# Strassen's seven products in the second feed-forward product of the last two token groups

## The chip, the cores and the metric

One core of one Trainium2 chip. The metric is the device time of one execution in microseconds (us), lower is better. In what follows PE is TensorE (its matmuls; PEld its weight loads), DVE is VectorE, ACT ScalarE, POOL GpSimd and SP SyncE, whose queue issues all the DMA transfers here. PSUM is the memory that matmuls write, eight banks of 512 float32 columns; SBUF is the working memory.

## The reference

Two branches on the same normalised input are added to the input: a spectral filter and a two-stage mixer.

```python
def _A_ref(x, w_r, w_i):                      # spectral filter
    X = rfft2(x)
    return irfft2(X * (w_r + 1j * w_i), (S, D))

def _B_ref(x, w1, w2, w3, w4):                # mixer
    h = gelu(layernorm(x) @ w1)               # then four channel quarters shifted by +1, -1, +2, -2 tokens
    x1 = x + concat(g0, g1, g2, g3) @ w2
    h2 = gelu(layernorm(x1) @ w3) @ w4        # the feed-forward part
    return x1 + h2

xn = layernorm(A_x)
out = A_x + _A_ref(xn, A_w_r, A_w_i) + _B_ref(xn, B_w1, B_w2, B_w3, B_w4)
```

There are S = 2048 tokens of D = 448 channels; w3 is 448 x 1792 (F = 1792), w4 is 1792 x 448. All is float32.

## The kernel before

**Precision.** Each float32 operand of a product is split into a high and a low half in float16 (a ScalarE copy gives the high half, a subtraction the low one), and a product is made of three passes: high by high, high by low, low by high (`PASS`). Powers of two from `powers` keep the halves in range.

**Tiles and groups.** The tokens are 16 tiles of 128 (b = 0 to 15, interleaved: token a * 16 + b). The feed-forward part works on groups G = 0 to 7 of two tiles each, 256 tokens.

**A unit.** For a group, the 1792 inner channels are taken in seven units fp = 0 to 6 of two blocks of 128 (f = 2 fp and 2 fp + 1). A unit has two halves.
- `front(G, fp)`: the product with w3 into one PSUM bank, [inner channel, token], by `mlp_in` (L381: 22 matmuls of 256 columns). Then Gelu in place in PSUM (L694, ScalarE), the high half (L696, ScalarE), the low half (L697, VectorE), into the tile `hf`.
- `back(G, fp)`: the product with w4, [token, output channel]; for each of the two token tiles and each of the two blocks three passes, added into the accumulators of the group, one bank for each tile (L716: 12 matmuls of 448 columns). In group 7 the second tile's accumulator is two halves of 224 columns in two banks, so its back is 6 matmuls of 448 and 12 of 224. At the group's last unit VectorE adds the accumulators to the residual (L728); for groups 6 and 7 (L723) it adds them to a row that already holds the rest of the output (`unscaled`, L493: a row of x loaded by SP, times and plus), and SP sends the result out (L725).

`mlp` runs the units of the groups that it is given, the front of a unit `ahead` units before its back (one for groups 3 to 7, two for 0 to 2).

**What else runs in the last 130 us.** The inverse transform, tile by tile: `gather_u` copies the transform's array `Y` of pool `pa2` for eight tiles into `U` (L651, VectorE, twice); `inv_a` has matmuls into a bank of tag `tr` (L659), a ScalarE copy (L663), two GpSimd sums (L666, L667), four VectorE sums (L668 to L671) and the split (L673, L674); `inv_b` is the second product (L681) and its addition to the tile (L682); `finish` loads a row of x, adds (L493) and sends the row out (L497).

**PSUM.** Four tags of two banks each: `mm` (fronts), `acc` (accumulators), `tr` (transposes, `inv_a`), `sp` (`inv_b` and group 7's third accumulator).

**SBUF.** `x2mem` holds the transposed input of all fronts (groups 0 and 1 in its first quarter, 2 and 3 in the second, 4 and 5, 6 and 7) and a strip behind them. `w4p` has the halves of w4. The four rows of groups 6 and 7 that hold the rest of the output lie in the first quarter.

**What sets the order.** The kernel text gives every engine's instructions with priorities: evictions first (`prio(EVAC)`), then the normal text in its order, feed-forward products last (`prio(FILL)`). A planner goes through them on a timeline of its own, takes on each engine the ready instruction of best priority, and so writes one fixed order for each engine, with all waits. On the chip, each engine goes through its order and waits where it must; nothing is reordered there.

## Time and profile before

| | us |
|---|---|
| time, median of 3 runs (lowest to highest) | 418.66 (418.37 to 418.75) |
| profiled execution: span from first to last instruction | 417.1 |
| median less span | 1.56 |
| PE busy | 408.7 (98%) |
| VectorE busy | 292.4 (70%) |
| ScalarE busy | 248.3 (60%) |
| GpSimd busy | 119.5 (29%) |
| L381, products with w3, 1232 matmuls | 152.2 |
| L716, products with w4, 714 matmuls | 140.0 |
| granted TensorE clock, mean | 0.999 |

For the profiled execution the page gives the span alone, so its own time is taken as the span and the 1.56 us around it. Matmuls are pipelined, so the busy times and mean durations of PE overlap each other; its pace is read from the starts of successive groups of matmuls. Times in a row of a timeline are the start and the length of a run of like instructions, in us from the start of the span; in brackets stands idle time of that engine ahead of the row and what ended it. In rows of groups, the two figures behind the first bar are the busy time in all (us) and the mean of one instruction (ns), behind the second bar the idle time ahead of them.

### The profile page before, as it was taken

Reading aid. Unit: us, or ns where it says so; the run is one execution under the profiler, and the core shown is the slowest. Engines: PE = TensorE matmul, PEld = TensorE weight load, DVE = VectorE, ACT = ScalarE, POOL = GpSimd, SP = SyncE. Lnnn points to the kernel's source line nnn. Section 1 sums busy time; section 2 is a strip of 40 time slices with the busy share of each in tenths; the row PEclk is TensorE's granted clock in tenths of the full one; section 3 lists DMA queues with packets and bytes.
Section 4 is the critical chain, followed back from the end, with each engine's and each line's share of the span. In section 5 each row is a group of like instructions: output and inputs, shape, how many; then the busy total and the mean of one; then the engine's idle time right before and its main releaser. Section 6 shows DMA issues by size and latency. Waiting matters only on the chain.

```text
span 417.1 us, 8522 instructions
## 1 busy us (share of the span) xinstructions
PE 408.7 (98%) x3313; PEld 290.1 (70%) x3313; DVE 292.4 (70%) x619; ACT 248.3 (60%) x428; POOL 119.5 (29%) x204
## 2 busy tenths in 40 slices
PE   8999999999999999999999999999999999999996
PEld 3655555765667777776887887777776767577885
DVE  4888899798774757643689889865999429942122
ACT  4698879963758866632678888864534415422321
POOL 3876810101246746300031221211354203200000
PEclk9999999999999999999999999999999999999999
DMA  8959879814961374305056565710002003331001
GB/s 269 344 196 176 159 152 328 158 45 96 214 135 45 90 259 142 110 24 140 13 154 168 144 150 139 181 33 2 2 2 75 14 2 133 134 132 46 2 0 46
DMA packets 55544, 48.53 MB, mean 116 GB/s; under 512 B 37648, under 2 KB 50768, under 8 KB 55504
## 3 DMA queue, kind: packets, MB, share of 16 engines
q1 hardware_dynamic: 55504, 47.99, 43.4%
q8 instruction: 26, 0.43, 0.4%
q14 instruction: 14, 0.11, 0.1%
HBM read 35.52 MB, written 3.67 MB: 94 GB/s over the span
## 4 chain that ended last, share of the span: by engine, by line
PE 63%; DVE 18%; DMA 6%; issue 6%; ACT 3%; POOL 2%; SPq 1%; DVEq 0%; POOLq 0%; ACTq 0%
PE pw L381 23%; PE acc L716 22%; PE pw L410 4%; PE ps L536 3%; PE pu L638 2%; PE pp L593 2%; PE px L610 2%; PE wps L752 2%; DVE xt L452 2%; DMA x2mem<-y 1%; DMA x2mem<-w 1%; DVE hf L697 1%; DMA xr<-x 1%; DVE y L484 1%; DMA out<-xr 1%
## 5 line engine op out<-in xcount | busy, mean ns | idle before, releaser
L381 PE MATMUL pw<-x2mem,w3p 128*128 128x256 f16 x1232 | 152.2, 272 | 0.0
L716 PE MATMUL acc<-w4p,hf 128*128 128x448 f16 (+1 forms) x714 | 140.0, 341 | 1.1 <-DVE hf L697 1.1
L381 PEld LDWEIGHTS <-w3p 128*128 128x128 f16 x1232 | 118.9, 98 | 23.5 <-issue 0.9
L716 PEld LDWEIGHTS <-hf 128*128 128x128 f16 x714 | 69.2, 98 | 49.4 <-DVE hf L697 1.9
L697 DVE SCALAR_TENSOR_TENSOR hf<-pw,h,hf 128x512 f16<-128x512 f32 x56 | 41.8, 747 | 56.4 <-ACT hf L696 56.1
L694 ACT ACTIVATE pw<-pw,pe 128x512 f32<-128x512 f32 x56 | 36.7, 655 | 69.9 <-PE pw L381 68.8
L450 PE MATMUL pw<-w2p,h 112*128 112x448 f16 x192 | 39.9, 352 | 0.9 <-DMA h<-hs 0.8
L696 ACT ACTIVATE hf<-pw,h 128x512 f16<-128x512 f32 x56 | 38.3, 686 | 1.4
L619 POOL TENSOR_TENSOR z<-te 128x450 f32<-128x450 f32 x16 | 16.3, 1016 | 74.0 <-DVE te L617 74.0
L410 PE MATMUL pw<-w1p,xT 128*128 128x448 f16 x176 | 35.4, 352 | 0.0
L450 PEld LDWEIGHTS <-h 112*128 112x128 f16 x192 | 18.6, 98 | 17.4 <-DMA h<-hs 1.1
L666 POOL TENSOR_TENSOR e<-e 128x226 f32<-128x226 f32 x16 | 13.8, 866 | 56.2 <-ACT e L663 45.0
L410 PEld LDWEIGHTS <-xT 128*128 128x128 f16 x176 | 17.0, 98 | 16.4 <-DVE xT L375 0.8
L600 ACT ACTIVATE pf<-pp 64x450 f16<-64x450 f32 x32 | 17.3, 541 | 16.6 <-DVE pf L601 8.1
L601 DVE TENSOR_TENSOR pf<-pp,pf 64x450 f16<-64x450 f32 x32 | 19.9, 621 | 5.3 <-ACT pf L600 5.0
L663 ACT ACTIVATE e<-pe 128x452 f32<-128x452 f32 x16 | 8.7, 548 | 15.9 <-DVE vh L674 11.9
L516 POOL TENSOR_TENSOR xr<-xf 128x452 f32<-128x452 f32 x8 | 9.5, 1194 | 28.5 <-issue 23.0
L615 ACT ACTIVATE te<-px 64x450 f32<-64x450 f32 x32 | 17.2, 539 | 0.5
L673 ACT ACTIVATE vh<-e 128x448 f16<-128x448 f32 x16 | 9.2, 574 | 13.3 <-DVE e L671 11.3
L519 POOL TENSOR_TENSOR f<-xr 128x452 f32<-128x452 f32 x16 | 16.1, 1029 | 0.6
L527 DVE TENSOR_TENSOR xh<-f,xh 128x452 f16<-128x452 f32 x16 | 11.8, 781 | 5.9 <-ACT xh L526 5.9
L681 PE MATMUL py<-vh,csm 128*128 128x448 f16 x48 | 13.5, 352 | 1.5 <-DVE vh L674 0.7
(166 smaller groups left out, 600.9 us busy)
## 6 DMA issues: line engine op xcount, KB each, us to landing
wc<-wf SPq DMA_DIRECT2D x32, 225.0 KB, 3.7
wl<-wf SPq DMA_DIRECT2D x8, 450.0 KB, 3.7
xt<-x SPq DMA_DIRECT2D x8, 448.0 KB, 8.5
xf<-x SPq DMA_DIRECT2D x8, 448.0 KB, 3.7
w3raw<-w SPq DMA_DIRECT2D x3, 896.0 KB, 12.9
xr<-x SPq DMA_DIRECT2D x12, 224.0 KB, 2.6
out<-xr SPq DMA_DIRECT2D x12, 224.0 KB, 2.0
gn<-c_g SPq DMA_DIRECT2D x16, 128.0 KB, 3.3
```

The lines of the kernel that those rows point to most:

```text
L381: T.matmul(ps_out, wp[:, wi + t, cols], xT[:, xi + t, tok], start=t == 0 and wi + xi == 0, stop=t == 3 and wi == 4)
L410: T.matmul(pm[:, :D], xTs[g][:, xi + t, 128 * i:128 * i + 128], w1p[:, wi + t], start=t == 0 and p == 0, stop=t == 3 and p == 2)
L450: T.matmul(pm[:, :D], hT[g][:112, 4 * hi + k, o:o + 128], w2p[:, wi, k], start=n == 0, stop=n == 11)
L519: P.tensor_tensor(out=f[:, :, k:k + 2].rearrange("p b s d -> p s b d"), in0=u[:, :, 0], in1=u[:, :, 1], op=op)
L600: A.activation(out=hi, in_=src, func=AF.Copy)
L601: V.tensor_tensor(out=lo, in0=src, in1=hi, op=ALU.subtract)
L615: A.activation(out=e[64 * h:64 * h + 64], in_=px_[64 - 64 * h:128 - 64 * h, :2 * DF], func=AF.Copy)
L619: P.tensor_tensor(out=z, in0=t[:, 0], in1=t[:, 1], op=ALU.add)
L694: A.activation(out=pm, in_=pm, func=AF.Gelu_apprx_tanh, scale=r3)
L696: i = A.activation(out=h[:, 0], in_=pm, func=AF.Copy, scale=h3)
L697: j = V.scalar_tensor_tensor(out=h[:, 1], in0=pm, scalar=h3, in1=h[:, 0], op0=ALU.mult, op1=ALU.subtract)
L716: m = T.matmul(to, h[:, hi, o:o + 128], w4p[0][:, wi, f, r], start=f == 0 and n == 0, stop=f == 13 and n == 2)
```

## The change

For eleven units (group 6: units 0 to 5; group 7: units 0 to 4) the back is a product of two by two blocks: two token tiles by two blocks of inner channels, times two blocks of inner channels by two halves of the output channels (`DH` = 224). It is done with seven products in place of eight, each in three passes: 21 matmuls of 224 columns.

- **Sums of activations** (`sums`): Gelu writes to SBUF in place of PSUM, GpSimd makes the sums (two instructions, 256 and 384 columns), and the split goes over seven blocks, 896 columns, in place of four.
- **Sums of weights** (`w4_sums`): for six units the two blocks of w4 are loaded from memory once more, GpSimd makes the four sums (three instructions), and they are split. The results go to parts of `x2mem` that groups 0 to 3 used, and to a strip behind `w4p`. Their working buffers are in a new pool `pz`, in the place of `pa2`, which is closed after the inverse transform's text.
- **Products** (`seven`): three of the seven go into the group's accumulators, four into two side banks of tag `tr`. After the group's last such unit VectorE adds the side banks, blocks repeated by a broadcast, to the rows of the output in five instructions; then the accumulators are evicted as before.
- **Order**: group 6 begins with its plain unit 6; group 7 ends with its plain units 5 and 6. `mlp` for groups 6 and 7 runs two fronts ahead in place of one. The rows that hold the rest of the output move to the input of groups 4 and 5, the third quarter of `x2mem`. `powers` leaves one bit more room for w4.

```diff
+DH = D // 2
+STR = {6: [6, 0, 1, 2, 3, 4, 5]}
+ORD = {G: STR.get(G, list(range(7))) for G in range(8)}
+SEVEN = {6: range(0, 6), 7: range(0, 5)}
...
@@ front
         with prio(EVAC):
+            if fp in SEVEN.get(G, ()):
+                hs[G, fp] = sums(G, fp, pm)
+                return
             A.activation(out=pm, in_=pm, func=AF.Gelu_apprx_tanh, scale=r3)
...
+    def sums(G, fp, pm):
+        g = pz.tile([128, 12, 128], F32, tag="g", bufs=2, name=f"g{G}{fp}")
+        q = g.rearrange("p (a r) n -> p a r n", r=3)
+        A.activation(out=q[:, 0:2, 0:3:2].rearrange("p t f n -> p f t n"),
+                     in_=pm.rearrange("p (f t n) -> p f t n", f=2, t=2), func=AF.Gelu_apprx_tanh, scale=r3)
+        P.tensor_tensor(out=q[:, 2:4, 0], in0=q[:, 0:2, 0], in1=q[:, 0:2, 2], op=ALU.add)
+        P.tensor_tensor(out=q[:, 0:3, 1], in0=q[:, 1:4, 0], in1=q[:, 0:3, 0], op=ALU.subtract)
+        h = pz.tile([128, 2, 7 * 128], F16, tag="hz", bufs=3, name=f"hz{G}{fp}")
+        src = g[:, 1:8].rearrange("p a n -> p (a n)")
+        A.activation(out=h[:, 0], in_=src, func=AF.Copy, scale=h3)
+        V.scalar_tensor_tensor(out=h[:, 1], in0=src, scalar=h3, in1=h[:, 0], op0=ALU.mult, op1=ALU.subtract)
+        return h
+
+    def w4_sums(j):
+        raw = pz.tile([128, 4, DH], F32, tag="wr", bufs=2, name=f"wr{j}")
+        SY.dma_start(raw.rearrange("p (f k) n -> p f (k n)", f=2), w4v[:, 2 * j:2 * j + 2])
+        t = pz.tile([128, 4, DH], F32, tag="wt", bufs=1, name=f"wt{j}")
+        P.tensor_tensor(out=t[:, 0:2], in0=raw[:, 1:4:2], in1=raw[:, 0:2], op=ALU.subtract)
+        P.tensor_tensor(out=t[:, 2], in0=t[:, 1], in1=raw[:, 0], op=ALU.add)
+        P.tensor_tensor(out=t[:, 3], in0=raw[:, 2], in1=t[:, 2], op=ALU.subtract)
+        split_w(w4t[j][:, 0], w4t[j][:, 1], t, s4)
+
+    def seven(G, fp):
+        h = hs.pop((G, fp))
+        f0, f1 = 2 * fp, 2 * fp + 1
+        if fp == SEVEN[G][0]:
+            side[G] = [bank("tr", f"side{G}{i}") for i in range(2)]
+        at1 = [acc[G][1][:, 0:DH], acc[G][2][:, 0:DH] if G == 7 else acc[G][1][:, DH:D]]
+        w = lambda f, k: [w4p[0][:, i, f, DH * k:DH * k + DH] for i in range(2)]
+        t = lambda k: [w4t[fp][:, i, k] for i in range(2)]
+        end = fp == SEVEN[G][-1]
+        for blk, to, b, first in ((2, side[G][0][:, 0:DH], w(f0, 0), True), (4, at1[0], w(f1, 0), None),
+                                  (1, acc[G][0][:, 0:DH], t(3), None), (6, at1[1], w(f1, 1), None),
+                                  (5, side[G][1][:, 0:DH], t(0), True), (3, side[G][0][:, DH:D], t(2), False),
+                                  (0, side[G][1][:, DH:D], t(1), False)):
+            for n, (hi, wi) in enumerate(PASS):
+                o = 128 * blk
+                m = T.matmul(to, h[:, hi, o:o + 128], b[wi], start=n == 0 and (first and fp == SEVEN[G][0] if first is not None
...
+        if end:
+            x = rest[2 * G][0].rearrange("p b (k n) -> p b k n", k=2)
+            m16, m57 = (t.rearrange("p (k n) -> p k n", n=DH) for t in (s[:, 0:D] for s in side[G]))
+            with prio(EVAC):
+                def add(to, m):
+                    V.scalar_tensor_tensor(out=to, in0=m, scalar=p34[:, 1:2], in1=to, op0=ALU.mult, op1=ALU.add)
+                flat4 = x.rearrange("p b k n -> p (b k) n")
+                wide = lambda m, n: m.unsqueeze(1).to_broadcast([128, n, DH])
+                add(flat4, wide(m16[:, 0], 4))
+                add(flat4[:, 0:2], wide(m16[:, 1], 2))
+                add(flat4[:, 3], m16[:, 1])
+                add(flat4[:, 1:4:2], wide(m57[:, 0], 2))
+                add(flat4[:, 0:2], wide(m57[:, 1], 2))
...
@@ mlp
-            todo = [(G, fp) for G in Gs for fp in range(7)]
+            todo = [(G, fp) for G in Gs for fp in ORD[G]]
...
-                if fp == 3 and last:
-                    for b in (2 * G, 2 * G + 1):
-                        rest[b] = unscaled(b, x2mem.bitcast(F32)[:, D * (b - 12):D * (b - 11)])
+                if fp == ORD[G][3] and last:
+                    both = x2mem.bitcast(F32)[:, D * (2 * G - 4):D * (2 * G - 2)].rearrange("p (b n) -> p b n", b=2)
+                    for i in range(2):
+                        rest[2 * G + i] = both, unscaled(2 * G + i, both[:, i])
...
-    w4p[0] = pa.tile([128, 2, 14, D], F16, tag="R", bufs=1, name="w4p")
+    w4mem = pa.tile([128, 8 * F], F16, tag="R", bufs=1, name="w4p")
+    w4p[0] = w4mem[:, 0:28 * D].rearrange("p (i f n) -> p i f n", i=2, f=14)
+    homes = [x2mem[:, F * k:F * k + F] for k in (0, 1, 2, 3, 8)] + [w4mem[:, 28 * D:28 * D + F]]
+    w4t.update({j: m.rearrange("p (i k n) -> p i k n", i=2, k=4) for j, m in enumerate(homes)})
...
-    mlp(range(6, 8), last=True)
+    close("pa2")
+    pz = pool("pz")
+    for j in range(6):
+        w4_sums(j)
+    mlp(range(6, 8), last=True, ahead=2)
```

37 lines of the change are left out of this document (23 added, 14 removed).

## Prediction

> **What bounds the kernel now.** The page was read first: its busy times, then the chain that ended last. After that came the table of busy times by stretch, the chain in order of time, and each engine's timeline around the last two token groups.
>
> ```profile
> span 417.1 us, 8522 instructions
> PE 408.7 (98%) x3313; PEld 290.1 (70%) x3313; DVE 292.4 (70%) x619; ACT 248.3 (60%) x428; POOL 119.5 (29%) x204
> 330.00:340.00 10.00, 10.00 (x76) 7.24 (x75) 1.56 (x3) 2.70 (x4) 0.00 (x0) 1.00 0.00 0
> 340.00:350.00 10.00, 10.00 (x72) 6.82 (x70) 7.16 (x12) 4.09 (x7) 0.33 (x1) 1.00 0.23 72
> 350.00:360.00 10.00, 10.00 (x89) 7.31 (x87) 9.17 (x20) 3.84 (x7) 6.00 (x8) 1.00 0.39 139
> 360.00:370.00 10.00, 9.58 (x65) 5.95 (x64) 7.84 (x19) 3.74 (x6) 0.00 (x0) 1.00 0.49 161
> 380.00:390.00 10.00, 10.00 (x83) 7.80 (x81) 2.69 (x4) 2.70 (x4) 0.00 (x0) 1.00 0.12 46
> ```
>
> The last five rows are ten-microsecond stretches: PE, PE loads, VectorE, ScalarE and GpSimd busy, granted clock, DMA. PE is full through nearly all of the last 75 us. VectorE's load is quite uneven: idle at 330 to 340, three quarters to nine tenths busy while the inverse transform's last tiles run (340 to 370), idle again behind that. So work taken off PE here shortens the kernel unless something new makes PE wait, and the stretch to fear is 340 to 370.
>
> The chain in order of time (start, length, what) gives PE's pace without the pipeline's overlap:
>
> ```profile
> 381.11 2.27 PE acc L716 x12
> 383.38 2.40 PE pw L381 x22
> 385.79 2.29 PE acc L716 x18
> 409.22 4.58 PE acc L716 x36
> ```
>
> A front (L381) is 22 products in 2.40 us. A back of group 6 is 12 products of 448 columns in 2.27 us, 189.2 ns each. In group 7 it is 6 of 448 and 12 of 224 in 2.29 us, so a product of 224 columns takes (2.29 - 6 x 0.1892) / 12 = 0.0962 us; the last 36, of which 12 are wide, give the same.
>
> The page's span is 417.1 us, the median of the runs 418.66: 1.56 us lie outside the span, and I carry them unchanged. From no change this measurement can tell about 0.2%, 0.84 us.
>
> **The products.** Eleven units (six of group 6, five of group 7) get seven products of blocks in three passes: 21 products of 224 columns, 21 x 0.0962 = 2.02 us. Group 6 gains 0.25 us in each, group 7 gains 0.27: 6 x 0.25 + 5 x 0.27 = 2.85 us, all of it on PE and on the path. The front is untouched. That is all that the change can win; everything else in it is cost.
>
> One thing could take this from the products: each brings a weight load of its own (98 ns in the groups' rows), now behind only 224 columns.
>
> ```profile
> L716 PEld LDWEIGHTS <-hf 128*128 128x128 f16 x714 | 69.2, 98 | 49.4 <-DVE hf L697 1.9
> 352.55 1.18 PE L659 MATMUL pe<-csm,U 113*128 113x113 f16 x20
> 353.57 1.15 PE L381 MATMUL pw<-x2mem,w3p 128*128 128x256 f16 x9
> ```
>
> The inverse transform's products take a load each too, and 20 of them start within 353.57 - 352.55 = 1.02 us, 51 ns apart. So loads overlap one another, and at 96 ns they do not set the pace. The Trainium skill, "TensorE: Matmul & The Clock Gate", section "LDWEIGHTS (loading the stationary operand)", puts a load at its columns over 1.2 per ns, an estimate of 106.7 ns for 128. If loads of that length were the pace, a unit would take 2.24 us and the gain would shrink to 6 x 0.03 + 5 x 0.05 = 0.43 us. The 51 ns speak against that.
>
> **The sums of activations.** A unit's eviction was Gelu, Copy and a subtraction of 512 columns. It becomes Gelu, two sums on GpSimd (256 and 384 columns), Copy and subtraction of 896 columns.
>
> ```profile
> L697 DVE SCALAR_TENSOR_TENSOR hf<-pw,h,hf 128x512 f16<-128x512 f32 x56 | 41.8, 747 | 56.4 <-ACT hf L696 56.1
> L694 ACT ACTIVATE pw<-pw,pe 128x512 f32<-128x512 f32 x56 | 36.7, 655 | 69.9 <-PE pw L381 68.8
> L696 ACT ACTIVATE hf<-pw,h 128x512 f16<-128x512 f32 x56 | 38.3, 686 | 1.4
> L666 POOL TENSOR_TENSOR e<-e 128x226 f32<-128x226 f32 x16 | 13.8, 866 | 56.2 <-ACT e L663 45.0
> L519 POOL TENSOR_TENSOR f<-xr 128x452 f32<-128x452 f32 x16 | 16.1, 1029 | 0.6
> L264 ACT ACTIVATE w4p<-x2mem,pe 128x896 f16<-128x896 f32 x7 | 6.8, 1030 | 2.7 <-DVE pe L251 2.7
> L265 DVE SCALAR_TENSOR_TENSOR w4p<-x2mem,pe,w4p 128x896 f16<-128x896 f32 x7 | 7.9, 1137 | 0.0
> ```
>
> Before: 0.66 + 0.69 + 0.75 = 2.1 us from front to back. After: Gelu 0.66, the sums 0.9 and 0.98 (between the rows of 226 and 452 columns), Copy 1.03, subtraction 1.14: 4.7 us. With two fronts ahead, two fronts and two backs lie between (2 x (2.40 + 2.02) = 8.8 us), so it is hidden; with one ahead, 4.4 us would not have hidden it, and every unit would have lost 0.3 us. Each unit adds 1.9 us to GpSimd, 0.34 to ScalarE, 0.39 to VectorE.
>
> **The sums of weights.** Six times: load 448 KB, three GpSimd sums (448, 224, 224 columns: 1.03 + 2 x 0.87 = 2.8 us), ScalarE 1.03, VectorE 1.14. The buffer between them is single, so they run one after the other, 5.0 us each, 30 us in all. They start when the pool they live in is free, that is when the second gather has read the transform's array.
>
> ```profile
> 308.65 2.77 DVE L651 COPY U<-y 113x1024 f16<-113x1024 f16 x8
> xf<-x SPq DMA_DIRECT2D x8, 448.0 KB, 3.7
> L493 DVE SCALAR_TENSOR_TENSOR x2mem<-xt,s,x2mem 128x448 f32<-128x448 f32 x4 | 3.2, 790 | 0.0
> 339.31 1.80 PE L381 MATMUL pw<-x2mem,w3p 128*128 128x256 f16 x15
> 355.12 2.24 PE L716 MATMUL acc<-w4p,hf 128*128 128x448 f16 x11
> ```
>
> From 311.4 + 3.7 = 315 us they need until 345 if nothing delays them, across VectorE's empty stretch at 330; their loads sit in SP's queue ahead of the row loads of the output, 3.7 us for each, where the DMA engines are mostly idle. The first is wanted near 355, where the second back of group 6 runs now (355.12), the others 4.4 us apart. So they cost nothing on PE while that stretch stays empty; at worst the last two slide behind 345. The four residual rows of groups 6 and 7 (L493 on x2mem, 4 x 0.79 = 3.2 us of VectorE) do move into the crowded stretch: their new place is the input of groups 4 and 5, which fronts read until shortly before 339.31, where the first front of group 6 stands.
>
> **VectorE and GpSimd meet.** On VectorE's and GpSimd's timelines:
>
> ```profile
> 311.82 0.96 POOL L667 TENSOR_TENSOR e<-e 128x226 f32<-128x226 f32 x1
> 312.27 1.00 DVE L674 TENSOR_TENSOR vh<-e,vh 128x448 f16<-128x448 f32 x1
> 313.93 0.74 DVE L697 SCALAR_TENSOR_TENSOR hf<-pw,h,hf 128x512 f16<-128x512 f32 x1
> 313.99 0.58 POOL L666 TENSOR_TENSOR e<-e 128x226 f32<-128x226 f32 x1 [1.20 <-ACT e L663]
> 315.37 0.61 DVE L674 TENSOR_TENSOR vh<-e,vh 128x448 f16<-128x448 f32 x1
> ```
>
> An L674 beside a GpSimd sum takes 1.00 us, alone 0.61: 0.39 us for each meeting. L697, which reads PSUM, takes 0.74 beside one too. The change moves that subtraction's input from PSUM to SBUF, so it becomes of the first kind. The Trainium skill, "SBUF — State Buffer", section "Who interferes with whom", says that a VectorE instruction with two SBUF inputs and a reading GpSimd instruction shut each other out for a whole instruction; the rows agree as to which instructions are hit, and by that rule a meeting could cost the whole 0.96 us of L667 in place of 0.39, and the 16 meetings below 15.4 us.
>
> For 340 to 370 VectorE has 7.16 + 9.17 + 7.84 = 24.2 us of work. To it come 3.2 (residual rows), five units x 0.39 = 2.0, and two late sums of weights, 2.3: 31.7 us in 30. With all 16 new GpSimd instructions there (five units of two, two of three) meeting one each, 6.2 more: 37.9. So the surplus is 1.7 to 7.9 us. The inverse tail, whose last output leaves at about 371, may end near 379, far ahead of the end; it is on the path only where PE waits in its written order, or where group 6's side sums wait for the two banks of the last inverse tile. To go on with, PE has the back of unit 6 and the fronts of units 2 and 3, about 7 us. PE waited 0.42 us in this stretch (10.00 - 9.58). On the gain side, taking the residual rows away from 298 to 313 could give back PE's waits there, seen in its timeline as 0.34 and 0.75 us (the third row is the inverse tail's last output):
>
> ```profile
> 298.60 0.54 PE L681 MATMUL py<-vh,csm 128*128 128x448 f16 x2 [0.34 <-ACT vh L673]
> 313.32 0.35 PE L681 MATMUL py<-vh,csm 128*128 128x448 f16 x1 [0.75 <-DVE vh L674]
> 369.52 1.51 SPq L497 DMA_DIRECT2D out<-xr  x2
> ```
>
> The price of this part lies between -1.1 and +4.8 us (the middle of the surplus, unhidden). I take +0.6, near the 0.42 that PE waits today, since fronts can fill in.
>
> **From group 6 to group 7.** Behind group 6's last product VectorE has five additions, then the two evictions that used to come alone.
>
> ```profile
> L723 DVE SCALAR_TENSOR_TENSOR x2mem<-acc,p,x2mem 128x448 f32<-128x448 f32 x3 | 2.0, 682 | 4.9 <-PE acc L716 4.9
> L723 DVE SCALAR_TENSOR_TENSOR x2mem<-acc,p,x2mem 128x224 f32<-128x224 f32 x2 | 0.9, 447 | 0.1
> 338.65 0.75 DVE L697 SCALAR_TENSOR_TENSOR hf<-pw,h,hf 128x512 f16<-128x512 f32 x1 [3.92 <-ACT hf L696]
> 340.94 0.92 PE L716 MATMUL acc<-w4p,hf 128*128 128x448 f16 x4
> ```
>
> The additions: one of 896 columns, 1.14 (L265 above; double the 448 row would be 1.36), three of 448 and one of 224: 1.14 + 3 x 0.68 + 0.45 = 3.63 us. With two evictions, 1.36, the accumulators of group 7 come free about 5.0 us after the last product. The program puts one front (2.40 us) between, so PE would wait 2.5 us. But its order is drawn up by a planner that takes what is ready: at 339.31 fifteen products of the next group's front stand ahead of the back of the unit whose activations land at 339.4. The same move, one more front (2.40), leaves 0.2 us. Bounds 0 and 2.5; I take 0.3.
>
> **The tail.** Today's last evictions:
>
> ```profile
> 412.68 1.60 DVE L723 SCALAR_TENSOR_TENSOR x2mem<-acc,p,x2mem 128x448 f32<-128x448 f32 x3 [1.25 <-PE acc L716]
> ```
>
> Group 7's additions start 4.58 us before PE ends (two plain units follow) and take 3.63, after which come the evictions of the last two tiles. Tile 14's eviction, which starts 1.1 us before PE's end (413.8 - 412.7), may be held for 0.2 us, and the last half tile for as much: 0 to 0.3, I take 0.15.
>
> **Sum.** -2.85 + 0.6 + 0.3 + 0.15 = -1.8: span 415.3, time **416.9 us**. Own range: from -2.85 - 0.35 (some of the earlier waits given back), 415.5, to 417.9 (1 us more of waits).
>
> **Rivals.** (1) *VectorE becomes the bound between 340 and 370*, the slower end. Its surplus there, 4.8 us in the middle, is paid by PE with at most one front as cover: 2.4 to 4.8, 3.6 in the middle, in place of 0.6: 418.66 - 2.85 + 0.45 + 3.6 = 419.9 us. For it: VectorE's 9.17 of 10, the 0.39 us meetings, and that group 6's side sums need banks of the last inverse tile. Against: 7 us of other PE work, and VectorE's empty stretch just before. It decides from 3.2 us of PE waits on. (2) *The step from group 6 to 7 is not filled*: 2.5 in place of 0.3, 416.9 + 2.2 = 419.1 us, not to be told from no change. Against: the planner's move at 339.31. (3) *Loads set the pace*: by the 98 ns of the load rows a unit takes 2.06 us, and the gain is 6 x 0.21 + 5 x 0.23 = 2.4 us: 417.3. The 51 ns between the inverse transform's products speak against it. By the Trainium skill's estimate for a load, above, it would be 419.3. (4) *The change does not shorten PE*, because something else sets the end: the inverse tail's last output leaves at 371, nothing else is near, so I leave it out.
>
> **Numbers.** Forecast 0.60, rival 1 0.25, rival 2 0.12, rival 3 0.03. Faster by over 0.2%: forecast and rival 3 by its rows, less a little for a forecast that pays 1 us more: 0.62. Slower: rival 1, 0.25. Within: rival 2 and the rest, 0.13. The likeliest is 416.9; the range goes from its low end, 415.5, to 420.2, just over rival 1's middle.
>
> **What would show it.** Right: backs of 21 products at 2.02 us; PE's busy stretches from 340 on with under 1.5 us of idle time; one or two extra fronts between group 6's last back and group 7's first; subtractions of 896 columns at 1.1 us, some at 1.5. Wrong: backs of 2.2 us (loads), waits of several us on PE ahead of group 6's first seven products with an inverse tile or VectorE as releaser (rival 1), or one wait of over 2 us behind the five additions (rival 2).

## The result, and the profile after

The changed kernel takes 423.65 us (median of 4 runs, 423.12 to 423.83) beside 418.71 us for the kernel before on the same chip (418.37 to 419.18): a ratio of 1.0116, interval 1.0102 to 1.013, slower by 4.9 us. The profiled execution of it took 423.12 us. Its page and its ten-microsecond stretches (PE, PE loads, VectorE, ScalarE, GpSimd, granted clock, DMA):

```profile
span 421.3 us, 8742 instructions
PE 408.6 (97%) x3382; PEld 297.1 (71%) x3382; DVE 318.4 (76%) x635; ACT 258.0 (61%) x434; POOL 152.9 (36%) x244
310.00:320.00 10.00, 8.68 (x83) 6.17 (x80) 9.03 (x20) 4.78 (x9) 6.23 (x9) 1.00 0.62 200
320.00:330.00 10.00, 8.07 (x77) 6.09 (x74) 8.91 (x14) 4.27 (x7) 7.54 (x10) 1.00 0.27 79
330.00:340.00 10.00, 9.53 (x56) 5.99 (x57) 4.59 (x7) 4.67 (x6) 5.01 (x7) 0.83 0.33 92
360.00:370.00 10.00, 8.84 (x88) 7.29 (x87) 10.00 (x20) 4.91 (x8) 5.93 (x8) 1.00 0.38 120
370.00:380.00 10.00, 8.85 (x80) 7.38 (x78) 9.19 (x16) 3.82 (x5) 5.17 (x6) 1.00 0.41 135
```

The same stretches of the kernel before that the prediction did not show:

```profile
310.00:320.00 10.00, 9.04 (x86) 6.60 (x85) 10.00 (x25) 3.49 (x6) 5.53 (x6) 1.00 0.07 25
320.00:330.00 10.00, 10.00 (x95) 7.29 (x93) 7.36 (x20) 5.17 (x9) 3.87 (x6) 1.00 0.24 70
370.00:380.00 10.00, 10.00 (x77) 7.24 (x75) 2.83 (x4) 2.70 (x4) 0.00 (x0) 1.00 0.13 48
```

The loss begins 30 us earlier than the prediction looked for it. PE is short of work in two places, 310 to 330 and 360 to 380, and runs at 0.83 of its clock between them. GpSimd, empty at 330 to 340 before, is busy for 5.01 us there now.

To see how much each place costs, one instruction is looked up in both PE timelines: a front product of group 5 behind its neighbour's back, and the first front piece behind the last back of group 5. Before:

```profile
292.79 0.27 PE L381 MATMUL pw<-x2mem,w3p 128*128 128x256 f16 x1
343.32 1.91 PE L381 MATMUL pw<-x2mem,w3p 128*128 128x256 f16 x16
```

After:

```profile
291.83 0.27 PE L385 MATMUL pw<-x2mem,w3p 128*128 128x256 f16 x1
348.07 2.13 PE L385 MATMUL pw<-x2mem,w3p 128*128 128x256 f16 x18
412.77 4.73 PE L787 MATMUL acc<-w4p,hf 128*128 128x448 f16 x36
```

The end of VectorE's timeline, after:

```profile
413.04 3.73 DVE L759 SCALAR_TENSOR_TENSOR x2mem<-side,p,x2mem 128x896 f32<-128x896 f32 x5
416.87 1.40 DVE L795 SCALAR_TENSOR_TENSOR x2mem<-acc,p,x2mem 128x448 f32<-128x448 f32 x3
```

Up to 292 us the changed kernel is 0.96 us ahead, with the same products behind it. Nearly all of that is a wait of 0.85 us that the kernel before has at 120 us, where nothing of the change stands; whether the planner's order or this one execution makes the difference is not shown. Up to the end of group 5 it goes from 0.96 ahead to 4.75 behind: 5.7 us lost, some 0.65 of it six front products (of 22 in 2.40 us) that stand earlier now, all other products being the same. From there to PE's end, 413.8 before and 417.5 after (412.77 + 4.73), it wins back 1.05 us. Behind PE's end come 3.8 us where there were 3.3: the five additions on the side banks run until 416.8, and the last evictions, which used to start 1.1 us before PE's end, start 0.6 us before it. -0.96 + 5.7 - 1.05 + 0.5 = 4.2 us, the difference of the two spans.

The largest piece, 5.7 us, can be followed between 309 and 334 us. First the load of weights in the chain in order of time, then VectorE's timeline, then GpSimd's, then PE's (in square brackets the idle time before, and who ended it):

```profile
309.14 3.10 DMA wr<-w
```

```profile
324.98 0.64 DVE L672 TENSOR_TENSOR e<-e 128x113 f32<-128x113 f32 x1 [1.09 <-POOL e L670]
326.12 1.47 DVE L269 SCALAR_TENSOR_TENSOR x2mem<-wt,pe,x2mem 128x896 f16<-128x896 f32 x1
327.70 1.23 DVE L675 TENSOR_TENSOR e<-e 128x111 f32<-128x111 f32 x1
329.68 0.74 DVE L704 SCALAR_TENSOR_TENSOR hf<-pw,h,hf 128x512 f16<-128x512 f32 x1
330.52 0.26 DVE L675 TENSOR_TENSOR e<-e 128x111 f32<-128x111 f32 x1
```

```profile
312.37 1.45 POOL L728 TENSOR_TENSOR wt<-wr 128x448 f32<-128x448 f32 x1 [0.56 <-DMA wr<-w]
324.37 0.58 POOL L670 TENSOR_TENSOR e<-e 128x226 f32<-128x226 f32 x1
327.67 1.13 POOL L728 TENSOR_TENSOR wt<-wr 128x448 f32<-128x448 f32 x1 [1.03 <-DVE x2mem L269]
```

```profile
316.63 0.54 PE L685 MATMUL py<-vh,csm 128*128 128x448 f16 x2 [1.14 <-ACT vh L677]
330.47 3.65 PE L787 MATMUL acc<-w4p,hf 128*128 128x448 f16 x10 [2.40 <-DVE hf L704]
```

The first load lands at 312.24, and the planner put the first three units' sums of weights (L728 to L730, L268, L269) at once between 312 and 332, where four inverse tiles (0 to 3) need GpSimd and VectorE too. Two things happen to an inverse tile there. It stands in GpSimd's queue: one tile's copy on ScalarE was done at 323.47, but its first GpSimd sum (L670) comes behind three sums of weights and starts at 324.37, and VectorE waits 1.09 us for it. And it meets GpSimd: a sum of a tile on VectorE (L675) that takes 0.26 us alone takes 1.23 beside GpSimd's sum of weights. Into VectorE's queue comes the subtraction of the second split (L269), 1.47 us. Behind all these, in VectorE's written order, stands an ordinary low half of group 5 (L704): its ScalarE half was done at 326.75, it starts at 329.68, and PE waits 2.40 us for it. Then PE's clock drops. The one-microsecond stretches have it at 0.50 in each of the three from 331 to 334, of which this is the first:

```profile
331.00:332.00 1.00, 1.00 (x4) 0.38 (x3) 0.53 (x1) 0.98 (x2) 0.00 (x0) 0.50 0.52 65
```

The ten products behind the wait take 3.65 us; the same ten behind the same wait, in a kernel where the clock stayed up (below), take 2.06. The wait of 1.14 us at 316.63 is hardly a loss, since the kernel before idles 0.96 us in the same stretch. By the stretches shown, PE's idle time from 310 to 340 grows from 0.96 to 3.72 us, by 2.8; with the 1.6 us of the slow clock 4.4 us have their rows. The 0.7 us left of the 5.7, beside the six products, are not divided further.

What the change was made for did happen. The back of a unit of group 7 in the chain in order of time:

```profile
402.09 0.29 PE side L750 x3
402.38 0.86 PE acc L750 x9
403.24 0.86 PE side L750 x9
```

21 products of 224 columns in 0.29 + 0.86 + 0.86 = 2.01 us.

### The profile page after: what moved, and what is told of

Read it like the earlier page. It is cut to its first block, busy times and chain, and to the rows that moved or that the text cites. A ratio compares the mean times of both kernels' runs of the same rounds, so it can differ in the third digit from the quotient of the medians.

```text
span 421.3 us, 8742 instructions
## 1 busy us (share of the span) xinstructions
PE 408.6 (97%) x3382; PEld 297.1 (71%) x3382; DVE 318.4 (76%) x635; ACT 258.0 (61%) x434; POOL 152.9 (36%) x244
## 4 chain that ended last, share of the span: by engine, by line
PE 58%; DVE 20%; issue 6%; ACT 5%; POOL 4%; DMA 4%; SPq 1%; DVEq 0%; POOLq 0%; ACTq 0%
PE pw L385 22%; PE acc L787 16%; PE pw L414 4%; PE ps L540 3%; PE pu L642 2%; PE pp L597 2%; PE px L614 2%; PE side L750 2%; PE wps L825 2%; PE acc L750 2%; DVE xt L456 2%; DVE hf L704 1%; DMA x2mem<-w 1%; DVE y L488 1%; DVE e L672 1%
## 5 line engine op out<-in xcount | busy, mean ns | idle before, releaser
L787 PE MATMUL acc<-w4p,hf 128*128 128x448 f16 (+1 forms) x552 | 114.0, 352 | 2.5 <-DVE hf L704 2.4
L787 PEld LDWEIGHTS <-hf 128*128 128x128 f16 x552 | 53.9, 98 | 43.4 <-DVE hf L704 3.5
L704 DVE SCALAR_TENSOR_TENSOR hf<-pw,h,hf 128x512 f16<-128x512 f32 x45 | 33.5, 746 | 23.4 <-ACT hf L703 22.9
L701 ACT ACTIVATE pw<-pw,pe 128x512 f32<-128x512 f32 x45 | 29.4, 653 | 26.2 <-PE pw L385 26.2
L703 ACT ACTIVATE hf<-pw,h 128x512 f16<-128x512 f32 x45 | 30.7, 685 | 1.1
L750 PEld LDWEIGHTS <-hz 128*128 128x128 f16 x231 | 22.2, 98 | 1.9 <-issue 1.0
L719 ACT ACTIVATE hz<-g,h 128x896 f16<-128x896 f32 x11 | 11.4, 1039 | 17.6 <-POOL g L716 17.6
L720 DVE SCALAR_TENSOR_TENSOR hz<-g,h,hz 128x896 f16<-128x896 f32 x11 | 13.8, 1257 | 10.4 <-ACT hz L719 10.4
L670 POOL TENSOR_TENSOR e<-e 128x226 f32<-128x226 f32 x16 | 10.8, 675 | 28.8 <-ACT e L667 17.6
L667 ACT ACTIVATE e<-pe 128x452 f32<-128x452 f32 x16 | 8.7, 548 | 18.5 <-DVE vh L678 14.4
L715 POOL TENSOR_TENSOR g<-g 128x256 f32<-128x256 f32 x11 | 9.1, 830 | 27.8 <-ACT g L713 27.8
```

Of the source, the lines that this page charges most:

```text
L701: A.activation(out=pm, in_=pm, func=AF.Gelu_apprx_tanh, scale=r3)
L703: i = A.activation(out=h[:, 0], in_=pm, func=AF.Copy, scale=h3)
L704: j = V.scalar_tensor_tensor(out=h[:, 1], in0=pm, scalar=h3, in1=h[:, 0], op0=ALU.mult, op1=ALU.subtract)
L750: m = T.matmul(to, h[:, hi, o:o + 128], b[wi], start=n == 0 and (first and fp == SEVEN[G][0] if first is not None else fp == ORD[G][0] and ...
L787: m = T.matmul(to, h[:, hi, o:o + 128], w4p[0][:, wi, f, r], start=first and f == 2 * fp and n == 0, stop=end and f % 2 == 1 and n == 2, s ...
```

## The experiments

Four theories were tried first, under these letters. **A**: the sums of weights, by their place (312 to 332) or by the work itself, disturb the inverse transform. **B**: the residual rows, moved to another part of SBUF, delay something. **C**: the products with their side accumulators give the 2.85 us, and all the rest is the price of the sums. **D**: the side accumulators' two banks, taken from the inverse transform, cost time.

**The residual rows alone.** The kernel before with the one line of the diff that moves them.

```diff
-  rest[b] = unscaled(b, x2mem.bitcast(F32)[:, D * (b - 12):D * (b - 11)])
+  rest[b] = unscaled(b, x2mem.bitcast(F32)[:, D * (b - 4):D * (b - 3)])
```

> The kernel before with one thing changed: the four rows with the rest of the output of groups 6 and 7 lie in the input of groups 4 and 5, as in the changed kernel, so they move from 298 to 312 us to behind 340 us. Theory A: 418 to 419.2 us, no difference to be told. Theory B: this move is the something else, 421 us or more.

Measured: 418.42 us, ratio 0.999 (0.998 to 1.0). B falls: the rows cost nothing.

**The products alone.** Seven products and the side additions, plain evictions, no sums of either kind.

```diff
-            if fp in SEVEN.get(G, ()):
-                hs[G, fp] = sums(G, fp, pm)
-                return
...
-        t = lambda k: [w4t[fp][:, i, k] for i in range(2)]
+        t = lambda k: w([f0, f0, f1, f1][k], k % 2)
...
-    for j in range(6):
-        w4_sums(j)
```

> Only the 21 products of 224 columns and the additions of the side banks: no sums of weights and no sums of activations; the evictions are the plain ones of 512 columns and the products read those, so the output is another one. Theory C (all that is lost behind 350 us is lost to the sums of activations on GpSimd, ScalarE and VectorE): the gain of the products less the tail, -2.85 + 0.6: 415.8 to 417.2 us. Theory D (the loss behind 350 us comes from where the products write: the side banks are those of the inverse tiles, PE waits for them in its order): 419 us or more.

Measured: 415.14 us, 0.9913 (0.9892 to 0.9934), faster by 3.6 us. Its stretch at 360 is full, where the changed kernel has 8.84 and the kernel before 9.58:

```profile
360.00:370.00 10.00, 10.00 (x94) 8.95 (x94) 7.76 (x16) 3.81 (x6) 0.00 (x0) 1.00 0.50 159
```

C holds, D falls. The gain is a little over 2.85 us because the waits that the kernel before has at 310 to 320 and 360 to 370 (0.96 and 0.42 us) are gone too, as the prediction's lower end allowed. From here on, 0.9913 is the mark: whatever a variant lacks to it is what the sums cost, with the order that the planner writes for them.

**The sums of weights alone.** The changed kernel with all products plain, in the order of before; the sums of weights are made and not used.

```diff
-STR = {6: [6, 0, 1, 2, 3, 4, 5]}
-SEVEN = {6: range(0, 6), 7: range(0, 5)}
+STR = {}
+SEVEN = {6: (), 7: ()}
...
-    mlp(range(6, 8), last=True, ahead=2)
+    mlp(range(6, 8), last=True)
```

> Plain products in all groups and one front ahead, as before the change, but the six sums of weights are still loaded, summed and split (nothing reads them). Theory A: they alone cost what the changed kernel lost before group 6, 3 to 6 us: 422 to 424.5 us. Theory B: within 0.8 us of the kernel before, 418 to 419.5 us.

Measured: 423.42 us, 1.0106 (1.0091 to 1.0121), so 4.4 us by themselves. Its PE timeline has the changed kernel's wait of 2.40 us again:

```profile
331.38 2.06 PE L787 MATMUL acc<-w4p,hf 128*128 128x448 f16 x10 [2.40 <-DVE hf L704]
```

**Is it their place?** The changed kernel with these sums held until the inverse sums of tile 3, the last of those four, are done on both engines (tiles 4 to 7 follow).

```diff
-        P.tensor_tensor(out=uf[:, 1], in0=e[:, 0:226], in1=e[:, 226:452], op=ALU.subtract)
+        i = P.tensor_tensor(out=uf[:, 1], in0=e[:, 0:226], in1=e[:, 226:452], op=ALU.subtract)
...
-        V.tensor_tensor(out=v[:, 225:336], in0=u[:, 1, 0, 1:112], in1=u[:, 1, 1, 1:112], op=ALU.add)
+        j = V.tensor_tensor(out=v[:, 225:336], in0=u[:, 1, 0, 1:112], in1=u[:, 1, 1, 1:112], op=ALU.add)
+        after["i", b] = i.ins, j.ins
...
-    for j in range(6):
-        w4_sums(j)
+    with behind("i", 3):
+        for j in range(6):
+            w4_sums(j)
```

> The changed kernel with the sums of weights held back: GpSimd's and VectorE's instructions for them are put behind the inverse transform's sums of tile 3, the last tile before VectorE's empty stretch, so that they run from about 327 us on. Theory A (the sums of weights in VectorE's crowded stretch at 312 to 331 delay the evictions, PE waits 2.4 us in one piece and its clock halves behind that): PE waits less than 1.5 us between 292 us and the end of group 5, the granted clock stays at 1.0, time 418 to 419.5 us. Theory B (the loss before group 6 comes from something else that was moved, not from the sums of weights): the loss stays, 423 us or more.

Measured: 423.59 us, 1.0106 (1.009 to 1.0123). The first loss was gone and a new one stood at 340 to 376. A stretch of it, and GpSimd's, ScalarE's and PE's rows in it:

```profile
350.00:360.00 10.00, 6.94 (x67) 5.09 (x64) 10.00 (x14) 4.37 (x7) 9.84 (x11) 1.00 0.44 140
```

```profile
352.52 1.52 POOL L729 TENSOR_TENSOR wt<-wr 128x448 f32<-128x448 f32 x1
355.00 1.43 POOL L670 TENSOR_TENSOR e<-e 128x226 f32<-128x226 f32 x1
356.39 0.96 POOL L671 TENSOR_TENSOR e<-e 128x226 f32<-128x226 f32 x1
```

```profile
353.54 0.53 ACT L667 ACTIVATE e<-pe 128x452 f32<-128x452 f32 x1
```

```profile
360.15 0.54 PE L686 MATMUL py<-vh,csm 128*128 128x448 f16 x2 [3.20 <-ACT vh L678]
```

Here GpSimd is full (9.84 of 10), VectorE too. The inverse tile's copy (L667) is done at 354.07, but its first GpSimd sum stands behind sums of weights, starts at 355.00 and takes 1.43 us, its second 0.96, where each took 0.58 when nothing met it (row of before, in the prediction). Every step of that tile is late, and PE waits 3.20 us for it. A smaller part comes through SP's queue: the residual rows' loads go out from 336.60, behind three loads of weights that hold the queue until 336.55, VectorE waits 2.10 us for the first of them at 340, and PE 0.97 us behind that. So the place alone isn't it: the same work, moved to where the activations' sums stand, costs the same.

**Two buffers.** The same with two buffers between the sums of weights and their split (`bufs=2` for the tile `wt`).

> The changed kernel with the sums of weights held back until the inverse transform's sums of tile 3 are through, and with two buffers for them in place of one, so that they follow each other at about 2.5 us and not 5. Theory A2 (whatever the sums of weights add to VectorE and GpSimd while inverse tiles run is paid by PE; VectorE's empty stretch at 327 to 342 us has room for all six): PE waits under 1.5 us up to 350, what stays is the loss of the kernel without them: 419.8 to 421.2 us. Theory B2 (their place does not matter, only their amount): 423 us or more.

Measured: 424.51 us, 1.0133 (1.0115 to 1.0151): a miss, the theory had a gain. The sums now waited for their loads, and the loads held up others behind them in SP's queue. GpSimd's and VectorE's rows:

```profile
331.22 1.14 POOL L729 TENSOR_TENSOR wt<-wr 128x448 f32<-128x448 f32 x1 [3.02 <-DMA wr<-w]
```

```profile
341.61 1.05 DVE L497 SCALAR_TENSOR_TENSOR x2mem<-xt,s,x2mem 128x448 f32<-128x448 f32 x1 [2.79 <-DMA x2mem<-x]
```

**Fewer units.** Seven products in group 7 alone, units 0 to 4 (five sums of weights, two buffers, held behind tile 3), and then units 0 to 3 with four sums of weights behind the inverse sums of tile 7, the last.

```diff
-STR = {6: [6, 0, 1, 2, 3, 4, 5]}
-SEVEN = {6: range(0, 6), 7: range(0, 5)}
+STR = {}
+SEVEN = {6: (), 7: range(0, 5)}
...
```

> Seven products only in group 7, units 0 to 4, behind the last inverse tile; group 6 plain, in the order 0 to 6; five sums of weights, held back and with two buffers; two fronts ahead for groups 6 and 7. Theory A2: the sums of activations meet no inverse tile, so the gain is 5 x 0.27 = 1.35 less the tail's 0.5, and the sums of weights cost 0 to 1: 417.3 to 418.8 us, faster than the kernel before or the same. Theory B2: the sums of weights cost 4 us wherever they are: 421 us or more.

> Seven products in group 7's units 0 to 3 alone; their four sums of weights are held back until the last inverse tile's sums are through (about 360 us), with two buffers; three plain units hide the additions. Theory S: nothing of the change meets an inverse tile, so the gain of four units stays, 4 x 0.27 = 1.1 us, with no tail: 417.3 to 418.1 us. If the sums of weights cost wherever they are: 419 us or more.

Measured: 419.11 us, 1.0004 (0.9993 to 1.0015), and 419.87 us, 1.0027 (1.0016 to 1.0038). Both miss: the first lies between its two theories, the second in the range of the theory that had no gain. In the second, PE still waited 1.44 us for ScalarE's vh and 1.23 us for VectorE's, at 363 and 365: "behind the last tile's sums" is not behind the tile's remaining steps, and other tiles' splits and row additions were still to come. Beside the held kernel with two buffers (1.0133) most of the loss is gone with group 6's units, but so is more than half of what the products can win, and neither kernel is faster than the one before.

**The activations' sums.** The changed kernel without any sums of weights (its products read w4's own halves), and then also without the two GpSimd sums of each unit (the Copy and the subtraction keep their 896 columns and read Gelu's output instead).

```diff
-        t = lambda k: [w4t[fp][:, i, k] for i in range(2)]
+        t = lambda k: w([f0, f0, f1, f1][k], k % 2)
...
-    for j in range(6):
-        w4_sums(j)
```

```diff
-        P.tensor_tensor(out=q[:, 2:4, 0], in0=q[:, 0:2, 0], in1=q[:, 0:2, 2], op=ALU.add)
-        P.tensor_tensor(out=q[:, 0:3, 1], in0=q[:, 1:4, 0], in1=q[:, 0:3, 0], op=ALU.subtract)
...
+        src = g[:, 2:3].to_broadcast([128, 7, 128])
```

> The changed kernel without the sums of weights: the seven products read slices of w4 itself in their place, so the output is another one; all else is kept. Theory A: no loss before group 6; what is left is the gain of the products, 2.85 us, less the waits in the crowded stretch behind 350 us (0.6 to 2) and the tail (0.6): 416.5 to 418.5 us. Theory B: 421 us or more.

> The changed kernel without the sums of weights and without GpSimd's two sums of each unit; Gelu into SBUF and the split of 896 columns stay (the seven blocks are all one block of Gelu's result, so the output is another one). If the waits behind 350 us come from GpSimd's sums shutting VectorE's instructions out and from the longer chain to the products: near the kernel with products alone, 416 to 417.5 us. If they come from VectorE's and ScalarE's longer instructions: near the kernel with the sums, 419.5 to 420.5 us.

Measured: 420.24 us, 1.0039 (1.0021 to 1.0058), a miss, and 415.82 us, 0.9925 (0.9907 to 0.9943). VectorE's and ScalarE's longer instructions cost next to nothing (0.9925 beside 0.9913, the intervals overlap); GpSimd's two small sums in each unit cost 1.1%, some 4.5 us, where there are no sums of weights at all. VectorE's split of the inverse tiles between 340 and 382, first with them, then without:

```profile
L678 DVE TENSOR_TENSOR vh<-e,vh 128x448 f16<-128x448 f32 x6 | 4.7, 783 | 0.0
```

```profile
L678 DVE TENSOR_TENSOR vh<-e,vh 128x448 f16<-128x448 f32 x6 | 3.6, 613 | 0.0
```

And PE's waits in the first of the two, both for an inverse tile:

```profile
364.01 0.54 PE L685 MATMUL py<-vh,csm 128*128 128x448 f16 x2 [1.91 <-ACT vh L677]
371.25 0.35 PE L685 MATMUL py<-vh,csm 128*128 128x448 f16 x1 [1.89 <-DVE vh L678]
```

**Meeting, or standing in the way?** Two things could do that: a GpSimd sum shuts VectorE out while it reads, or it only takes GpSimd's time and puts a longer chain between Gelu and Copy. So GpSimd's sums were replaced by fills of about the same length (0.74 and 0.95 us), which read nothing.

```diff
-        P.tensor_tensor(out=q[:, 2:4, 0], in0=q[:, 0:2, 0], in1=q[:, 0:2, 2], op=ALU.add)
-        P.tensor_tensor(out=q[:, 0:3, 1], in0=q[:, 1:4, 0], in1=q[:, 0:3, 0], op=ALU.subtract)
+        P.memset(g[:, 5:11], 0.5)
+        P.memset(g[:, 0:8], 0.25)
```

> The changed kernel without the sums of weights, and with GpSimd's two sums of each unit replaced by two fills of as long a duration (768 and 1024 columns, about 0.74 and 0.95 us), which read nothing from SBUF; the chain Gelu, GpSimd, Copy, subtraction stays as long (the output is another one). Theory S (shut out by GpSimd's reads): the time falls to that of the kernel without GpSimd's sums, 415.5 to 417 us. Theory L (the longer chain, or inverse sums that stand behind the new ones in GpSimd's order): it stays near the kernel with the sums, 419 to 420.5 us.

Measured: 419.43 us, 1.0003 (0.999 to 1.0016). VectorE's split is back at its length alone:

```profile
L678 DVE TENSOR_TENSOR vh<-e,vh 128x448 f16<-128x448 f32 x6 | 3.7, 614 | 0.0
```

Yet only about a third of the loss is gone: of 1.14% between the two kernels above, 0.36% goes with the reading, and 0.78% stays. These differences are of kernels from different chips, each against its own before, so the share is rough. What the 0.78% is, the run does not show. Of the four inverse tiles in this stretch only one stands behind a fill in GpSimd's queue, for 0.7 us. PE's three waits there (1.70, 1.12 and 0.79 us) are for inverse tiles that stand, in VectorE's order, behind a row addition of `finish` (L497) which waits 1.2 to 1.4 us for its load. The second of them, on VectorE's and PE's timelines (the tile's ScalarE half was done at 362.65):

```profile
364.32 0.69 DVE L497 SCALAR_TENSOR_TENSOR xr<-xt,s,xr 128x448 f32<-128x448 f32 x1 [1.38 <-DMA xr<-x]
```

```profile
365.59 0.35 PE L685 MATMUL py<-vh,csm 128*128 128x448 f16 x1 [1.12 <-DVE vh L678]
```

So a third thing stands beside the two: the loads of rows, in the order that the planner wrote for this kernel. No experiment here separates it from the time on GpSimd.

**The weights again.** The sums of weights alone, as above, but without GpSimd's part: ScalarE and VectorE split the raw load.

```diff
-        P.tensor_tensor(out=t[:, 0:2], in0=raw[:, 1:4:2], in1=raw[:, 0:2], op=ALU.subtract)
-        P.tensor_tensor(out=t[:, 2], in0=t[:, 1], in1=raw[:, 0], op=ALU.add)
-        P.tensor_tensor(out=t[:, 3], in0=raw[:, 2], in1=t[:, 2], op=ALU.subtract)
+        t = raw
```

> Plain products, one front ahead, and the six extra loads of w4 with their splits, but without GpSimd's sums (the split reads the load itself; nothing reads the results). Theory S (VectorE's instructions with two SBUF inputs and GpSimd's sums shut each other out, and that is most of the cost): well under the 423.4 us of the kernel that has GpSimd's sums of weights too, 418.5 to 420.5 us. Theory V (VectorE's and ScalarE's splits of 896 columns in the crowded stretch cost it): 422 to 424 us.

Measured: 421.64 us, 1.0057 (1.0042 to 1.0071), where it was 1.0106 with them. Between the two expectations: GpSimd's sums are about half of what the weights cost; the other half is the rest of that work, the loads and the splits in ScalarE's and VectorE's crowded queues, which this run does not part.

**All sums on VectorE.** If GpSimd's part in the chain is the loss, the same sums on VectorE should be cheaper, though VectorE is the fuller engine. This is the held kernel with five letters changed, nothing else:

```diff
-        P.tensor_tensor(out=q[:, 2:4, 0], in0=q[:, 0:2, 0], in1=q[:, 0:2, 2], op=ALU.add)
+        V.tensor_tensor(out=q[:, 2:4, 0], in0=q[:, 0:2, 0], in1=q[:, 0:2, 2], op=ALU.add)
...
```

> The whole change with all sums on VectorE in place of GpSimd, the sums of weights held back until the inverse transform's sums of tile 3. VectorE gets 0.9 us more for each unit and 1.3 us for each sum of weights. Theory S (being shut out costs more than VectorE's own time): below the changed kernel's 423.65, 417.5 to 420.5 us. Theory V (VectorE's time is what is short): 423 us or more.

Measured: 417.71 us, 0.9971 (0.996 to 0.9981), where it was 1.0106. A sum of 384 columns, on GpSimd in the held kernel and on VectorE in this one (lowest, median and highest duration in ns), and then the page's busy line and PE's timeline of this one:

```profile
L717 POOL TENSOR_TENSOR g<-g x11: 992/997/1727, 351.2 to 404.1; 128x384 f32<-128x384 f32 x11
```

```profile
L717 DVE TENSOR_TENSOR g<-g x11: 544/553/936, 350.9 to 397.9; 128x384 f32<-128x384 f32 x11
```

```profile
PE 405.4 (97%) x3382; PEld 296.3 (71%) x3382; DVE 326.1 (78%) x675; ACT 258.4 (62%) x434; POOL 118.5 (28%) x204
```

```profile
370.35 0.54 PE L686 MATMUL py<-vh,csm 128*128 128x448 f16 x2 [1.57 <-ACT vh L678]
```

VectorE is busy for 326.1 us, more than in any other kernel here, and the kernel is faster than the one before and the changed one. Of the waits at 340 to 376 only one, of 1.57 us, is left. So VectorE's time is not what was short. Which part of doing the sums on GpSimd costs the most is not parted by this: the longer instructions (1.00 us where VectorE takes 0.55), the queue there and the meetings go all at once.

**Which of the two kinds?** The held kernel with only the activations' sums on VectorE, and with only the weights' (two of the five letters are in the activations' sums, three in the weights').

> The changed kernel with the sums of the weights held behind the inverse sums of tile 3 and the sums of the activations on VectorE; the sums of the weights stay on GpSimd. All on GpSimd gave 1.0106 of the time before, all on VectorE 0.9971. Theory A (the activations' sums are what GpSimd delays, as the 4.4 us without any sums of weights say): 0.998 to 1.002, most of the gain kept. Theory W (the weights' sums, three long instructions a unit, are what delays): 1.006 to 1.010.

> The other way round: the sums of the weights on VectorE, those of the activations on GpSimd, held as before. Theory A: 1.006 to 1.010, since GpSimd still stands between Gelu and the split. Theory W: 0.998 to 1.002. If both kernels come out near the middle (1.003 to 1.006), the two kinds share the loss of 5.7 us.

Measured: 420.64 us, 1.005 (1.0035 to 1.0065), and 420.24 us, 1.0039 (1.0026 to 1.0052). The two kinds share the loss: 0.56% comes back with the one, 0.67% with the other, 1.35% with both (again each against its own before, on three chips).

**And the place, without GpSimd?** The changed kernel, nothing held, all sums on VectorE: five letters.

> The changed kernel with all its sums on VectorE and nothing held: the planner puts the sums of the weights where it likes. Theory place (the first sums of weights at 312 to 331 us cost by where they stand): 1.001 to 1.005, with waits of TensorE between 315 and 332 again. Theory engine (they cost because GpSimd does them): 0.996 to 0.999, as with them held.

Measured: 417.52 us, 0.9976 (0.9968 to 0.9985). The planner again put sums of weights at 312 to 332, and there one wait is left instead of the two:

```profile
326.93 0.77 PE L663 MATMUL pe<-csm,U 113*128 113x113 f16 x12 [1.08 <-ACT e L667]
```

Held or not makes no difference that these intervals tell (0.9971, 0.9976). The engine was what mattered, not the place.

**The tail.** All sums on VectorE, held, and one unit fewer in group 7, so that three plain units stand behind the additions.

```diff
-SEVEN = {6: range(0, 6), 7: range(0, 5)}
+SEVEN = {6: range(0, 6), 7: range(0, 4)}
```

> All sums on VectorE, sums of weights held, and group 7 with seven products in units 0 to 3 instead of 0 to 4, so that three plain units stand behind the side additions. Theory T (the tail of 0.64 us is the additions standing too late): one more plain unit costs 2.28 - 2.02 = 0.26 us, the tail gives back 0.3 to 0.6, so 0.995 to 0.997 against 0.9971 with five units. Rival (the tail is set by the last evictions and the store alone): 0.9975 to 0.9985, slower by the 0.26 us.

Measured: 416.31 us, 0.9945 (0.9932 to 0.9958), the fastest with the whole computation, and a little better than the range that was expected. VectorE's end:

```profile
404.92 1.40 DVE L760 SCALAR_TENSOR_TENSOR x2mem<-side,p,x2mem 128x448 f32<-128x448 f32 x2
410.64 1.60 DVE L796 SCALAR_TENSOR_TENSOR x2mem<-acc,p,x2mem 128x448 f32<-128x448 f32 x3 [3.54 <-PE acc L788]
```

The last additions are done at 406.3, well before PE's last products, VectorE waits 3.54 us for PE instead of PE's results waiting for VectorE, and the tail behind PE (its last 54 products end at 411.75, the span at 415.1) is 3.35 us, about as before the change. That is 0.45 us less than the 3.8 of the changed kernel and of the same kernel with five units, as expected. Less 0.26 us for the plain unit, it should win 0.2 us; the whole step, 0.26% or 1.1 us, is more. The profiled executions put the rest outside the edit: this one is ahead of the one with five units by 0.72 us already at 299 us, in a part that the edit does not touch (most of it the wait at 120 us, 0.91 here and 1.36 there), and from there on it gains 0.1 us. So the shorter tail is shown, and 0.9945 beside 0.9971 is not its price.

## Why the prediction was wrong, and where it was right

**Right: the products.** 2.01 us in each unit where 2.02 was worked out, and 3.6 us for the products alone with two old waits thrown in. The loads do not set the pace (rival 3). The residual rows cost nothing.

**Right: the step from group 6 to group 7.** PE waits nowhere there; the planner moved front products of group 7 in between, as at 339.31 before. After, on PE's timeline:

```profile
393.39 1.69 PE L385 MATMUL pw<-x2mem,w3p 128*128 128x256 f16 x14
395.49 1.04 PE L385 MATMUL pw<-x2mem,w3p 128*128 128x256 f16 x8
```

The term was 0.3 us; no wait stands there. Rival 2 did not come.

**Wrong: "they cost nothing on PE while that stretch stays empty".** The step that failed is putting the sums, of weights and of activations, at nothing on PE; this is the first half of it. I laid the weights' sums from 315 to 345, one behind the other, "across VectorE's empty stretch at 330", and asked only whether the last two come too late. They did stand there, but the first three, at 312 to 332, fell into a stretch whose VectorE share I never looked up: 10.00 of 10 at 310 to 320. All six cost 4.4 us by themselves. Moving them would not have saved the forecast: held back to the empty stretch, they cost as much further on.

**Wrong: "so it is hidden".** I compared the longer chain of an activation, 4.7 us, with 8.8 us of PE work, and that comparison holds: PE's five waits between 360 and 375 in the changed kernel, 2.3 us in all, are for the inverse transform, none for hz. But the new sums use the two engines that the inverse tiles use. One tile's copy was done at 357.36, and its first GpSimd sum starts at 358.66, behind a sum of activations; PE waited for those tiles. Hidden from its own consumer is not hidden from its neighbours in the queue. That is some 4.5 us in the kernel without sums of weights.

**Wrong in size: 0.39 us for a meeting.** Single meetings cost up to 0.97 us (L675, 1.23 beside 1.13 of GpSimd, 0.26 alone). The prediction put a rule of the Trainium skill beside it ("SBUF — State Buffer", section "Who interferes with whom"), that the two engines shut each other out for a whole instruction; these rows agree with the rule and not with my 0.39. The same section says that a GpSimd instruction that only writes does not do this, and the fills agree (614 ns beside them, 613 without, 783 beside the sums). But in the kernel with fills only about a third of the activations' loss is gone; the rest, queues and the written order, my sum had nowhere, since it counted work on GpSimd ("adds 1.9 us to GpSimd" in each unit) and gave it no price on PE.

**Too small: the inverse stretch and the tail.** The term of +0.6, with bounds to +4.8, came out at 2.3 us of waits at 360 to 375 where 0.42 had been, so 1.9, and, in the stretch that I had not looked at, at 5.1 (the 5.7 without the six products). The tail was 0.15, at most 0.3, and came out at 0.5. The additions were to start 4.58 us before PE's end; they start 4.46 before it (417.5 - 413.04), behind the low half of the last plain unit (L704), take 3.73 instead of 3.63, and the evictions behind them end at 418.27, 0.77 us behind PE, where it was 0.48 before. That is 0.29 of the 0.5; the rest lies between the last eviction and the end of the span.

**Rival 1** came nearest, inverse tiles that arrive late because VectorE is full and meets GpSimd, with a time of 419.9. It was 3.7 us short: it sat at 340 to 370, and most of the loss came at 312 to 334. With the sums of weights held, the whole loss did stand at 340 to 376, and was as large. Half of its mechanism fell: VectorE's time was not the bound, since the kernel in which VectorE has the most work is faster than the one before.

## What to carry to other kernels

Before moving small work to an idle engine, look at who is queued behind it there: in this kernel GpSimd was 29% busy, but its sums for the inverse tiles stood between two steps on other engines, and giving the new sums to VectorE, at 76% the fuller engine, was worth 1.35% in the held kernel. Where a planner fixes the order, ask for the busy shares at the earliest moment at which new work may start, since that is where it will be put; here that explains the place of the first loss, though holding the work back did not make it cheaper. And price the gain and each cost by a kernel that has only that one: here the products alone (0.9913) told at once that the idea was sound and its helpers were not.

## What the runs showed of the hardware

I had not expected the clock to fall at all. Behind the wait of 2.40 us at 330 the granted clock was 0.50 for about 3 us; behind the wait of 3.20 us in the held kernel it was 0.50 too, in two full one-microsecond stretches (the first is shown) and parts of two others:

```profile
362.00:363.00 1.00, 1.00 (x8) 0.80 (x6) 1.00 (x4) 0.00 (x0) 0.00 (x0) 0.50 0.00 0
```

Behind a wait of the same 2.40 us, in the kernel with the sums of weights alone, it stayed at full:

```profile
332.00:333.00 1.00, 1.00 (x7) 0.54 (x6) 0.63 (x1) 0.97 (x3) 0.00 (x0) 1.00 0.54 65
```

So the length of the wait alone does not decide it, and what does is not shown. The Trainium skill, "TensorE: Matmul & The Clock Gate", section "HAM oscillation — how this bites in real kernels", gives gaps above about 3.4 us as the ones to avoid; here 2.40 us was enough once, and 3.20 us the other time.
